# Building kv transposed from split features, and streaming five weight tiles instead of two

## The chip, the cores and the metric

The kernel runs on one core of a Trainium2 chip. The metric is the device time of one execution in microseconds (us). The names of the engines in this document: PE is TensorE (matmuls), PEld its weight loads, DVE is VectorE, ACT is ScalarE, POOL is GpSimd, SP is SyncE, which issues all the DMAs here. SBUF is the on-chip memory of 128 partitions, PSUM the eight banks that PE writes into.

## The reference

It is a linear attention with positive random features, followed by a mixer and an MLP. All is fp32 (U, V and the MLP weights arrive as float64 words).

```python
def phi(x):                                   # q, k: [8, 8, 576, 64], w_phi: [64, 128]
    proj = einsum('bhsd,df->bhsf', x, w_phi)
    proj = proj - max(abs(proj), axis=-1)
    return concatenate([exp(proj), exp(-proj)], axis=-1)     # 256 features
q_p, k_p = phi(q), phi(k)
kv  = einsum('bhsf,bhsd->bhfd', k_p, v)       # [256 features, 64] per head
z   = sum(k_p, axis=2)                        # [256 features] per head
x   = (q_p @ kv) / (q_p @ z + 1e-6)           # then [8, 576, 512]
u   = x + (x^T U V)^T                         # U: [576, 32], V: [32, 576]
out = u + relu(u @ w_ch1) @ w_ch2             # [512, 2048], [2048, 512]
```

The change is about kv and z: for each head, 576 rows of 256 features against 64 columns of v, and the sum of those features.

## The kernel before, in words

**Attention.** Work goes by pairs of heads: eight batches b of four pairs, 32 pairs in all. Of the 576 rows 512 are the main part (NT = 4 tiles of 128) and 64 the tail; the tails of a pair's two heads are done together. Pairs of batches 0 and 1 are unsplit; from batch 2 on (`SPLIT`, L247) a pair is split: q and k are cut into a high part in fp32r, a rounded format, and a low part, the rest in fp32r, and products are made from those parts.

A pair passes through steps (L494 to L519): `s_project_k0` and `s_project_k1` make the k features of the two heads (tiles kp0, kp1: 128 rows x 4 tiles x 256 features, and kpt for the tail); `s_project_q0` and, inside `s_kv0_q1`, `project_q(1)` make the q features, transposed, with a maximum over partitions on POOL (`partition_all_reduce`, L363). kv is built in `kv_tail` (L432) and `kv_main` (L440): v carries a 65th column of ones (`vb`, `vt`, L104 to L115), so that one matmul gives kv and z. In `kv_main` the weights are 128 features (fp32), the moving operand 65 columns of v (fp32): per head 4 tiles x 2 halves of the features = 8 matmuls, all into one PSUM bank, `kv_ps`, held from `kv_tail` to `kv_done` (L447), where DVE copies it out. `s_out0` and `s_out1` (L514, L518) take q's features against kv and divide.

**The mixer and the MLP.** `Tokens` (L527) does U and V for a batch, stores u to DRAM (`u_dram`), and `Mixer.load_blocks` (L600) reads it back in blocks of 32, which `turn_blocks` turns on DVE and splits into `uT_hi` and `uT_lo`. The MLP goes over nine groups g of 512 rows (eight batches and the eight tails), each in sixteen blocks f of 128 hidden units (`Mixer.chunks`, L672): `hidden(f)` is 12 matmuls of 128x512 in fp32r into the bank `ph` (one buffer), which ACT reads as `h_hi` (L624) and then DVE as `h_lo` (L625); `add(f)` is 12 matmuls into four banks `o`. The order is hidden(0), hidden(1), add(0), hidden(2), add(1) and so on.

**The weights.** Each w1 and w2 block is converted once from its float64 words (`convert_block`, L215) while batch 0 and 1 run, split into high and low part and then kept in SBUF, 4 KB a partition for one tile (`home`, a tag per tile). Two blocks, f = 0 and f = 8 (`STREAM`, L188), are also stored to DRAM (`kept`) and later share the home of f = 0: after the last use of the one in a group, `stream` (L198) loads the other from `kept`. Two blocks, f = 8 and f = 15 (`WHOLE`), have homes that other tiles use as well: y of `load_blocks` and the first x.

**The order.** The main loop (L848) runs over pairs: cur is in its output steps, nxt in its feature and kv steps, far has its transfers started, all of them on SP's queue. After each step, `Pace.step` (L719) lets in as many MLP chunks of the batch before as keeps pace: 28 of a group's 32 chunks over 34 steps; the last four (`HELD`) go in while the next group's u is turned. The program is traced in this order. The framework then puts each engine's instructions into a fixed order with a model of their times, and adds the semaphores. Each engine but PE's weight loads runs its own instructions strictly one after another.

PSUM has three banks `at` for attention (projections, kv_ps, xp, transposes), one `ph`, four `o`. Feature tiles have three buffers (`feat`), those of the tail two (`feat_t`), a pair's raw q and k two in all, v's tiles two sets, used by turns.

Of the kernel before, what the change touches and what calls it, by code (L numbers as in the profile page):

```python
# [9 lines left out]
F32 = mybir.dt.float32  # L10
F32R = mybir.dt.float32r
# [10 lines left out]
P = 128  # L22
# [3 lines left out]
def tile_kernel(  # L26
# [46 lines left out]
    def f32(ap):  # L73
        return ap.bitcast(F32)
# [109 lines left out]
    w1_t, w2_t, words, found = {}, {}, {}, {}  # L184
    LAST = NFC - 1

    WHOLE = {LAST: "w_last", 8: "w_late"}
    STREAM = (0, 8)  # L188
    kept = {f: dram.tile([P, 2, 2, C], F32, name=f"kept{f}") for f in STREAM}

    def place(f, dt, shape, name):

        if f in WHOLE:
            both = home.tile([P, 2, *shape], dt, tag=WHOLE[f], name=name)
            return both[:, 0], both[:, 1]
        return [home.tile([P, *shape], dt, tag=f"w{n}_{f}", name=f"{name}_{n}") for n in (1, 2)]

    def stream(n, g, f):  # L198

        to = STREAM[1 - STREAM.index(f)]  # L200
        if g == 0 or g == B and to == 0:
            return
        w = home.tile([P, 2, C], F32R, tag=f"w{n + 1}_0", name=f"w{n + 1}_{to}_{g}")
        nc.sync.dma_start(out=f32(w), in_=kept[to][:, n])
        (w1_t, w2_t)[n][to] = w
# [9 lines left out]
    def convert_block(i):  # L215
        f, n = divmod(i, 2)
        r = convert(words[f][n], f"w{n + 1}_{f}")
        if f not in WHOLE:
            w = home.tile([P, 2, C], F32R, tag=f"w{n + 1}_{f}", name=f"w{n + 1}_{f}")
            split_w((nc.scalar.copy, nc.vector.tensor_copy)[n], r, w)  # L220
        elif n == 0:
            found[f] = r
            return
        else:
            w1_w, w = place(f, F32R, (2, C), f"w_{f}")
            split_w(nc.scalar.copy, found[f], w1_w)
            split_w(nc.vector.tensor_copy, r, w)
            w1_t[f] = w1_w
        (w1_t, w2_t)[n][f] = w
        if f in STREAM:  # L230
            for i in range(2) if f in WHOLE else (n,):
                nc.sync.dma_start(out=kept[f][:, i], in_=f32((w1_t, w2_t)[i][f]))
# [16 lines left out]
    class Pair:  # L249
# [90 lines left out]
        def k_tile(self, n, ng):  # L340
            tag, bufs = ("feat", 3) if ng > 1 else ("feat_t", 2)
            return att.tile([P, ng, 2 * F], F32, tag=tag, bufs=bufs, name=f"kp{self.nm}_{n}")

        def k_features(self, n, k_w, kp):

            ng = kp.shape[1]
# [44 lines left out]
        def project_k_split(self, g):  # L391
# [3 lines left out]
            for s in range(2):  # L395
                pk = self.ps(f"pk{g}{s}_").rearrange("p (t n f) -> p t n f", t=2, n=2)
                for i in range(2):
# [4 lines left out]
                nc.scalar.copy(out=kp[:, ts_, 0:F], in_=pk[:, :, 1, :])  # L402
                nc.vector.tensor_tensor(  # L403
                    out=k_w[:, ts_, :], in0=pk[:, :, 0, :], in1=kp[:, ts_, 0:F], op=ALU.add)
            return self.k_features(g, k_w, kp)

        def project_q_tail(self):
            pq = self.ps("pqt")
# [23 lines left out]
        def kv_tail(self):  # L432
            self.kv_ps = self.ps("kv_ps", True)
            self.kv_v = self.kv_ps[:, 0:4 * (D + 1)].rearrange("p (f h e) -> p f h e", f=2, h=2)
            for f in range(2):
                nc.tensor.matmul(  # L436
                    self.kv_v[:, f, :, :], self.kpt[:, 0, f * F:(f + 1) * F], self.vt,
                    start=(f == 0), stop=False, skip_group_check=True)

        def kv_main(self, g, kp):  # L440
            for t in range(NT):
# [56 lines left out]
        def s_project_k1(self):  # L498
            self.kp1 = self.project_k(1)
            self.project_q_tail()  # L500

        def s_project_q0(self):
            self.qp0 = self.project_q(0)

        def s_kv0_q1(self):
            self.kv_tail()
            self.kv_main(0, self.kp0)
            self.qp1 = self.project_q(1)

        def s_kv1(self):  # L510
            self.kv_main(1, self.kp1)
            self.kv_done()

# [316 lines left out]
    if True:  # L830
# [16 lines left out]
        tk = Tokens(0, x, xt)  # L847
        for n, (b, j) in enumerate(pairs):  # L848

            far = Pair(*pairs[n + 2]) if n + 2 < len(pairs) else None  # L850
            if n < len(LOADS):

# [82 lines left out]
```

## Time and profile before

| what | us |
|---|---|
| median of 3 runs (1226.07 to 1227.72) | 1227.1 |
| the profiled execution | 1233.19 |
| its span, from the first to the last instruction | 1231.4 |
| PE busy in the span | 1204.2 |
| DVE busy | 690.9 |
| ACT busy | 538.2 |
| POOL busy | 203.6 |
| one batch from the third on (382.5 to 516.6) | 134.1 |

Busy time is the union of an engine's instructions. Matmuls are pipelined: their lengths overlap, so what one costs is read from the distance between starts. In rows of the timeline, `x4` means four instructions of one kind merged, and square brackets name the idle time of the engine ahead of the row and what ended it. In rows of groups, the two numbers behind the bar are busy us and the mean ns of one; behind the second bar stands idle time of the engine ahead of them. An unsplit fp32 matmul leaves two records, one for each of its passes.

### The profile page before, as it was taken

How to read it: one execution, taken by the hardware profiler on the slowest of the kernel's cores; microseconds unless marked ns; L12 is line 12 of the kernel's file. 1: busy time of each engine (PE TensorE's matmuls, PEld its weight loads, DVE VectorE, ACT ScalarE, POOL GpSimd, SP SyncE). 2: the span in 40 equal slices, each digit the busy share in tenths (PEclk: the TensorE clock that was granted, in tenths of full speed). 3: DMA queues.
4: the chain of work that ended last, by engine and by line, in shares of the span. 5: the costliest groups of instructions: out<-in, count | busy, mean ns of one | idle time of the engine just before them, and what ended most of it. 6: DMA issues, size and time to landing. Idle time of an engine off the chain costs nothing.

```text
span 1231.4 us, 18285 instructions
## 1 busy us (share of the span) xinstructions
PE 1204.2 (98%) x6667; PEld 1036.6 (84%) x6669; DVE 690.9 (56%) x1517; ACT 538.2 (44%) x1151; POOL 203.6 (17%) x154
## 2 busy tenths in 40 slices
PE   8999998999999999999999999999999999999997
PEld 7887787888888888888888888888888888888886
DVE  5857879775566656665647556655656543312111
ACT  6866678554543444444534444344434431111110
POOL 3533444211110111011111111011201110000000
PEclk9979999999999999999999999999999999999999
DMA  4766221331234213431244123421343015400201
GB/s 133 241 227 208 70 64 30 90 109 25 54 97 116 48 40 91 90 99 30 64 115 111 28 52 86 111 69 26 88 107 98 1 52 150 112 35 1 69 1 35
DMA packets 248345, 100.60 MB, mean 82 GB/s; under 512 B 215360, under 2 KB 227904, under 8 KB 248256
## 3 DMA queue, kind: packets, MB, share of 16 engines
q1 hardware_dynamic: 248256, 99.44, 31.2%
q8 instruction: 53, 0.87, 0.3%
q14 instruction: 36, 0.29, 0.1%
HBM read 78.41 MB, written 20.97 MB: 81 GB/s over the span
## 4 chain that ended last, share of the span: by engine, by line
PE 78%; DVE 8%; SPq 4%; ACT 4%; DMA 4%; issue 1%; POOL 0%; DVEq 0%; ACTq 0%; POOLq 0%
PE ph L619 27%; PE o L640 27%; PE kv_ps L443 7%; PE xp L482 7%; SPq L605 2%; SPq L265 2%; PE pk L399 2%; DVE w L236 1%; PE pp L561 1%; PE kv_ps L436 1%; PE pq L422 1%; DMA raw<-in_q_dram 1%; PE pq L423 1%; PE xpt L469 1%; DMA y<-u_dram 1%
## 5 line engine op out<-in xcount | busy, mean ns | idle before, releaser
L619 PE MATMUL ph<-uT_hi,w 128*128 128x512 f32 x1152 | 389.0, 395 | 4.7 <-DVE h_lo L625 3.3
L640 PE MATMUL o<-w,h_hi 128*128 128x512 f32 x1152 | 327.1, 395 | 3.2 <-ACT h_hi L624 3.2
L619 PEld LDWEIGHTS ph<-uT_hi,w 128*128 128x128 f32 x1152 | 216.2, 188 | 51.2 <-DVE h_lo L625 5.6
L640 PEld LDWEIGHTS o<-w,h_hi 128*128 128x128 f32 x1152 | 211.1, 188 | 45.3 <-ACT h_hi L624 4.9
L619 PE MATMUL ph<-uT_lo,w 128*128 128x512 f32 x576 | 225.1, 391 | 0.0
L624 ACT ACTIVATE h_hi<-ph 128x512 fp32r<-128x512 f32 x144 | 85.9, 596 | 272.0 <-PE ph L619 261.0
L625 DVE SCALAR_TENSOR_TENSOR h_lo<-ph,h_hi 128x512 fp32r<-128x512 f32 x144 | 98.6, 685 | 176.6 <-ACT h_hi L624 175.4
L640 PE MATMUL o<-w,h_lo 128*128 128x512 f32 x576 | 191.9, 395 | 0.6 <-DVE h_lo L625 0.6
L363 POOL PARTITION_ALL_REDUCE qp<-qp x64 | 126.7, 1980 | 286.6 <-ACT qp L362 268.1
L443 PEld LDWEIGHTS kv_ps<-vb,kp 128*128 128x128 f32 x1024 | 126.6, 195 | 2.8
L482 PEld LDWEIGHTS xp<-kv,qp 128*128 128x128 f32 x1024 | 124.1, 194 | 4.8 <-DVE kp L403 0.9
L619 PEld LDWEIGHTS ph<-uT_lo,w 128*128 128x128 f32 x576 | 108.3, 188 | 21.3 <-DVE uT_lo L244 0.6
L443 PE MATMUL kv_ps<-vb,kp 128*128 128x65 f32 x1024 | 126.0, 274 | 0.1
L482 PE MATMUL xp<-kv,qp 128*128 128x65 f32 x1024 | 124.0, 274 | 0.6 <-DVE kp L403 0.6
L640 PEld LDWEIGHTS o<-w,h_lo 128*128 128x128 f32 x576 | 105.4, 188 | 21.6 <-DVE h_lo L625 1.3
L353 ACT ACTIVATE kp<-kp 128x512 f32<-128x512 f32 x64 | 40.4, 632 | 132.9 <-DVE kp L350 83.4
L363 POOL PARTITION_ALL_REDUCE qp_t<-qp_t x32 | 27.2, 851 | 403.2 <-ACT qp_t L362 401.0
L319 DVE TENSOR_TENSOR T<-raw,T 64x512 fp32r<-64x512 f32 x96 | 68.5, 714 | 33.6 <-ACT T L318 31.1
L315 DVE STREAM_TRANSPOSE raw<-raw 128x512 f32<-128x512 f32 x48 | 34.1, 711 | 80.3 <-DMA raw<-in_q_dram 36.8
L318 ACT CAST T<-raw 64x512 fp32r<-64x512 f32 x96 | 59.3, 618 | 33.9 <-PE pq L423 23.4
L365 ACT ACTIVATE qp<-qp 128x512 f32<-128x512 f32 x64 | 40.4, 631 | 59.8 <-DVE qp L364 59.5
L146 POOL INT64_ADD w_ab<-w_ab x32 | 44.1, 1377 | 76.0 <-DVE w_ab L142 40.4
(128 smaller groups left out, 1357.1 us busy)
## 6 DMA issues: line engine op xcount, KB each, us to landing
words<-in_moe_w_ch_dram SPq DMA_DIRECT2D x32, 512.0 KB, 8.0
w<-kept SPq DMA_DIRECT2D x30, 512.0 KB, 4.1
vb<-in_v_dram SPq DMA_DIRECT2D x64, 128.0 KB, 2.5
u_dram<-x SPq DMA_DIRECT2D x32, 256.0 KB, 2.2
st<-u_dram SPq DMA_DIRECT2D x16, 512.0 KB, 4.0
out_dram<-st SPq DMA_DIRECT2D x32, 256.0 KB, 2.3
y<-u_dram SPq DMA_DIRECT2D x112, 64.0 KB, 2.4
raw<-in_k_dram SPq DMA_DIRECT2D x192, 32.0 KB, 2.0
```

Of the source, the lines that this page charges most:

```text
L146: nc.gpsimd.int64_add(a64, a64, b64)
L318: nc.scalar.copy(out=m[here, s, :], in_=x_[here])
L319: nc.vector.tensor_sub(m[there, s, :], x_[here], f32(m[here, s, :]))
L353: nc.scalar.activation(out=kp[:, :, 0:F], in_=kp[:, :, F:2 * F], func=AF.Exp)
L363: nc.gpsimd.partition_all_reduce(qp[:, 0, :], qp[:, 1, :], P, ReduceOp.absmax)
L365: nc.scalar.activation(out=qp[:, 0, :], in_=qp[:, 1, :], func=AF.Exp)
L443: nc.tensor.matmul(self.kv_v[:, f, g, :], kp[:, t, f * F:(f + 1) * F], self.vb[:, g, t, :], start=False, stop=(t == NT - 1), skip_group_ch ...
L482: nc.tensor.matmul(xv[:, c, :], qp[:, f, c * P:(c + 1) * P], self.kv[:, f, c // 2 if self.split else s, :], start=(f == 0), stop=(f == 1))
L619: nc.tensor.matmul(ph, w1_part(f, l, c), r[:, c, :], start=(n == 0), stop=(n == 3 * NCC - 1))
L624: on_act = nc.scalar.activation(out=h_hi, in_=ph, func=AF.Relu)
L625: on_dve = nc.vector.scalar_tensor_tensor(out=h_lo, in0=ph, scalar=0.0, in1=f32(h_hi), op0=ALU.max, op1=ALU.subtract)
L640: nc.tensor.matmul(self.o[t], l[:, cs], w2_t[f][:, r, :], start=(f == 0 and n == 0), stop=(f == NFC - 1 and n == 2))
```

## The change

For split pairs, kv is built the other way round, as 64 rows of v against 256 moving features, and in fp32r parts:

- v is split into high and low part, side by side as 128 weight columns (`v_parts`); the features into `khi` (ACT) and `klo` (DVE) (`k_parts`).
- `kv_turned` streams the features' two parts past v's two parts: per head 4 tiles x 2 parts = 8 matmuls of 128x256 into one bank `kt`. Its upper and lower 64 rows, from v's high and low part, are added into `kvT`.
- `kv_end`, at the head of the next pass of the main loop, turns `kvT` back with two transposes on PE, does the tail (`kv_tail`, which stood in `s_kv0_q1`), copies `kv_ps` out and adds the turned kv and the sums.
- The sums z of the main rows, which the ones column gave, come from `k_sums`: two adds on DVE, a sum over partitions on POOL, and a trip through DRAM (`zd`) that turns a row of 256 sums per head into columns (`k_sums_turned`).

Room for these tiles comes from the weights: five blocks (0, 3, 6, 9, 12) instead of two now share the home of f = 0 and are streamed one after another; the homes that blocks 3, 6 and 9 have during batch 0's group (`late0` to `late5`) then serve the tiles above. `w_late` holds block 12 instead of 8. Unsplit pairs run as before.

```diff
-    WHOLE = {LAST: "w_last", 8: "w_late"}
-    STREAM = (0, 8)
+    WHOLE = {LAST: "w_last", 12: "w_late"}
+    STREAM = (0, 3, 6, 9, 12)
...
+    def place_of(n, f):
+        if f in STREAM[1:]:
+            return f"late{2 * STREAM.index(f) - 2 + n}"
+        return f"w{n + 1}_{f}"
...
     def stream(n, g, f):
-        to = STREAM[1 - STREAM.index(f)]
+        to = STREAM[(STREAM.index(f) + 1) % len(STREAM)]
...
+        def k_sums(self, g, kp):
+            if g == 0:
+                self.zs = home.tile([P, 2, 2, 2 * F], F32, tag="late2", name=f"zs{self.nm}")
+                self.zd = dram.tile([2, 2 * F], F32, tag="zd", bufs=2, name=f"zd{self.nm}")
+            zs = self.zs[:, g]
+            nc.vector.tensor_add(zs, kp[:, 0:2, :], kp[:, 2:4, :])
+            nc.vector.tensor_add(zs[:, 0, :], zs[:, 0, :], zs[:, 1, :])
+            nc.gpsimd.partition_all_reduce(zs[:, 1, :], zs[:, 0, :], P, ReduceOp.add)
+            nc.sync.dma_start(out=self.zd[g:g + 1, :], in_=zs[0:1, 1, :])
+
+        def k_sums_turned(self):
+            self.zc = small.tile([P, 2, 2], F32, tag="zc", bufs=2, name=f"zc{self.nm}")
+            nc.sync.dma_start(
+                out=self.zc.rearrange("p g n -> p (g n)"),
+                in_=self.zd.rearrange("g (n f) -> f (g n)", f=F))
+
+        def k_parts(self, g, kp):
+            hi = home.tile([P, NT, 2 * F], F32R, tag=f"late{5 * g}", name=f"khi{self.nm}_{g}")
+            lo = home.tile([P, NT, 2 * F], F32R, tag="late1", name=f"klo{self.nm}_{g}")
+            nc.scalar.copy(out=hi, in_=kp)
+            nc.vector.tensor_sub(lo, kp, f32(hi))
+            return hi, lo
+
+        def v_parts(self):
+            self.v_hl = home.tile([P, 2, NT, 2 * D], F32R, tag="late3", name=f"v_hl{self.nm}")
+            src = self.vb[:, :, :, 0:D]
+            nc.scalar.copy(out=self.v_hl[:, :, :, 0:D], in_=src)
+            nc.vector.tensor_sub(
+                self.v_hl[:, :, :, D:2 * D], src, f32(self.v_hl[:, :, :, 0:D]))
+
+        def kv_turned(self, g, parts):
+            kt = self.kt = self.ps(f"kt{g}_")
+            for t in range(NT):
+                for n in range(2):
+                    nc.tensor.matmul(
+                        kt[:, 0:2 * F], self.v_hl[:, g, t, :], parts[n][:, t, :],
+                        start=(t == 0 and n == 0), stop=(t == NT - 1 and n == 1))
+            if g == 0:
+                self.kvT = home.tile([P, 2, 2 * F], F32, tag="late4", name=f"kvT{self.nm}")
+            r_ = slice(g * D, (g + 1) * D)
+            nc.scalar.copy(out=self.kvT[r_, 1, :], in_=kt[D:2 * D, 0:2 * F])
+            nc.vector.tensor_add(self.kvT[r_, 0, :], kt[0:D, 0:2 * F], self.kvT[r_, 1, :])
+
+        def kv_end(self):
+            if not self.split:
+                return
+            kb = self.kt[:, 2 * F:4 * F]
+            for f in range(2):
+                nc.tensor.transpose(
+                    out=kb[:, f * P:(f + 1) * P], in_=self.kvT[:, 0, f * F:(f + 1) * F],
+                    identity=ident)
+            self.kv_tail()
+            self.kv = small.tile([P, 2, 2, D + 1], F32, tag="kv", bufs=1, name=f"kv{self.nm}")
+            nc.vector.tensor_copy(out=self.kv, in_=self.kv_v)
+            nc.vector.tensor_add(
+                self.kv[:, :, :, 0:D], self.kv[:, :, :, 0:D],
+                kb.rearrange("p (f h d) -> p f h d", f=2, h=2))
+            nc.vector.tensor_add(
+                self.kv[:, :, :, D:D + 1], self.kv[:, :, :, D:D + 1],
+                self.zc.rearrange("p g n -> p n g").unsqueeze(3))
...
                 nc.vector.tensor_tensor(
                     out=k_w[:, ts_, :], in0=pk[:, :, 0, :], in1=kp[:, ts_, 0:F], op=ALU.add)
-            return self.k_features(g, k_w, kp)
+            self.k_features(g, k_w, kp)
+            self.k_sums(g, kp)
+            return kp
...
         def s_project_k1(self):
             self.kp1 = self.project_k(1)
             self.project_q_tail()
+            if self.split:
+                self.v_parts()
 
         def s_project_q0(self):
             self.qp0 = self.project_q(0)
+            if self.split:
+                self.parts0 = self.k_parts(0, self.kp0)
 
         def s_kv0_q1(self):
+            if self.split:
+                self.k_sums_turned()
+                self.kv_turned(0, self.parts0)
+                self.qp1 = self.project_q(1)
+                self.parts1 = self.k_parts(1, self.kp1)
+                return
             self.kv_tail()
             self.kv_main(0, self.kp0)
             self.qp1 = self.project_q(1)
 
         def s_kv1(self):
+            if self.split:
+                self.kv_turned(1, self.parts1)
+                return
             self.kv_main(1, self.kp1)
             self.kv_done()
...
         for n, (b, j) in enumerate(pairs):
 
+            cur.kv_end()
             far = Pair(*pairs[n + 2]) if n + 2 < len(pairs) else None
```

More of the change, by code (lines that the diff above doesn't have):

```diff
@@ L195, in place @@
             return both[:, 0], both[:, 1]
-        return [home.tile([P, *shape], dt, tag=f"w{n}_{f}", name=f"{name}_{n}") for n in (1, 2)]
+        return [home.tile([P, *shape], dt, tag=place_of(n, f), name=f"{name}_{n}") for n in (0, 1)]
     def stream(n, g, f):
-        to = STREAM[1 - STREAM.index(f)]
+        to = STREAM[(STREAM.index(f) + 1) % len(STREAM)]
         if g == 0 or g == B and to == 0:
@@ L218, in convert_block @@
         if f not in WHOLE:
-            w = home.tile([P, 2, C], F32R, tag=f"w{n + 1}_{f}", name=f"w{n + 1}_{f}")
+            w = home.tile([P, 2, C], F32R, tag=place_of(n, f), name=f"w{n + 1}_{f}")
             split_w((nc.scalar.copy, nc.vector.tensor_copy)[n], r, w)
@@ L437, in kv_tail @@
                     self.kv_v[:, f, :, :], self.kpt[:, 0, f * F:(f + 1) * F], self.vt,
-                    start=(f == 0), stop=False, skip_group_check=True)
+                    start=(f == 0), stop=self.split and f == 1, skip_group_check=True)
         def kv_main(self, g, kp):
```

## The prediction

> **What bounds the kernel now.** I read the page's busy times first, then busy time by windows, then the timeline of TensorE, then the waits.
>
> ```profile
> span 1231.4 us, 18285 instructions
> PE 1204.2 (98%) x6667; PEld 1036.6 (84%) x6669; DVE 690.9 (56%) x1517; ACT 538.2 (44%) x1151; POOL 203.6 (17%) x154
> ```
>
> The profiled execution took 1233.2 us, 1.8 us more than its span and 6.1 us more than the median of the runs (1227.1); I sum against 1233.2 and take 6.1 off at the end. A busy PE need not be a full one, so I ask stage by stage (columns: window, length, then busy PE, PEld, DVE, ACT, POOL).
>
> ```profile
> 80.00:248.00 168.00, 157.57 (x885) 133.18 (x886) 135.43 (x263) 118.62 (x234) 63.95 (x44) 0.99 0.33 97
> 382.50:516.60 134.10, 133.75 (x768) 116.74 (x767) 81.48 (x185) 59.89 (x133) 18.94 (x12) 1.00 0.33 76
> 650.70:784.80 134.10, 133.44 (x766) 116.24 (x766) 80.54 (x183) 59.51 (x132) 18.95 (x12) 1.00 0.32 75
> ```
>
> From about 248 us on a batch (four pairs of heads, sixteen MLP blocks) takes 134.1 us, and PE is idle in 0.35 to 0.66 us of it. DVE is busy 60%, ACT 45%. So in that stage PE time removed is time removed, until another engine takes PE's place. The timeline shows what a pair's kv costs there (start, length, instruction; starts follow each other without gaps, lengths overlap).
>
> ```profile
> 594.15 0.61 PE L436 MATMUL kv_ps<-vt,kp_t 128*128 128x130 f32 x4
> 594.60 1.90 PE L443 MATMUL kv_ps<-vb,kp 128*128 128x65 f32 x16
> 596.30 0.48 PE L422 MATMUL pq<-T,w_hl 128*128 128x512 f32 x1
> 596.62 0.40 PE L423 MATMUL pq<-T,w_hl 128*128 128x512 f32 x1
> 596.85 1.89 PE L443 MATMUL kv_ps<-vb,kp 128*128 128x65 f32 x16
> 598.55 0.48 PE L619 MATMUL ph<-uT_hi,w 128*128 128x512 f32 x1
> 598.87 0.40 PE L619 MATMUL ph<-uT_lo,w 128*128 128x512 f32 x1
> ```
>
> Eight program matmuls of one head are sixteen records: plain fp32 runs each in two passes. One head takes 596.30 - 594.60 = 1.70 us, the tail 0.45. The first 128x512 after such a stretch takes 0.32 us to the next start where the usual step is 0.23 (596.62 to 596.85): 0.09 us per stretch. A pair's kv: 0.45 + 2 x 1.70 + 2 x 0.09 = 4.03 us.
>
> **The change, PE part.** kv_turned takes 8 matmuls of 128x256 in fp32r per head; kv_end adds two 128x128 transposes; the two tail matmuls move there unchanged. The same shapes run already:
>
> ```profile
> 603.41 0.64 PE L399 MATMUL pk<-w_hl,T 128*128 128x256 f32 x4
> 603.89 0.40 PE L640 MATMUL o<-w,h_lo 128*128 128x512 f32 x1
> 244.17 0.60 PE L593 MATMUL pt<-ident,x 128*128 128x128 f32 x4
> 244.52 0.48 PE L577 MATMUL vp<-pst,v_all 128*128 128x512 f32 x1
> ```
>
> (603.89 - 603.41) / 4 = 0.12 us a matmul, single records, so 16 are 1.92 us. A transpose is (244.52 - 244.17) / 4 = 0.09 us; I take 0.10. One fp32 stretch is left: 0.09. Together 1.92 + 0.20 + 0.45 + 0.09 = 2.66 us, saved 1.37 us a pair. Batches 2 to 7 are split, 24 pairs: **32.9 us off PE**. A batch becomes 134.1 - 5.5 = 128.6 us if nothing else takes over.
>
> [...]
>
> ```profile
> L399 PEld LDWEIGHTS pk<-w_hl,T 128*128 128x128 f32 x192 | 31.2, 189 | 4.2
> ```
>
> **DVE, ACT, POOL.** Prices of the added work (count | busy us, mean ns):
>
> ```profile
> L350 DVE TENSOR_TENSOR kp<-kp,mk 128x512 f32<-128x512 f32 x48 | 33.1, 690 | 1.2
> L548 DVE TENSOR_TENSOR xs<-x,xs 128x256 fp32r<-128x256 f32 x64 | 27.2, 470 | 7.7 <-ACT xs L547 7.5
> L403 DVE TENSOR_TENSOR kp<-pk,kp 128x256 f32<-128x256 f32 x96 | 37.4, 409 | 2.0 <-ACT kp L402 2.0
> L456 DVE TENSOR_SCALAR den<-xp 128x4 f32<-128x4 f32 x64 | 10.2, 160 | 27.9 <-PE xp L482 27.2
> L353 ACT ACTIVATE kp<-kp 128x512 f32<-128x512 f32 x64 | 40.4, 632 | 132.9 <-DVE kp L350 83.4
> L402 ACT COPY kp<-pk 128x256 f32<-128x256 f32 x96 | 33.3, 371 | 35.0 <-PE pk L399 34.8
> L363 POOL PARTITION_ALL_REDUCE qp<-qp x64 | 126.7, 1980 | 286.6 <-ACT qp L362 268.1
> L363 POOL PARTITION_ALL_REDUCE qp_t<-qp_t x32 | 27.2, 851 | 403.2 <-ACT qp_t L362 401.0
> ```
>
> From 256 to 512 columns DVE adds about 0.27 us and ACT 0.26, so 128x1024 is near 1.23 and 1.15 us. DVE per pair: sums 2 x (0.69 + 0.47), lo parts 2 x 1.23, v's lo 0.69, kvT adds 2 x 0.41, the two last adds 0.41 + 0.16 (the copy out of kv_ps was there before): 6.9 us, 27 a batch. ACT: hi parts 2 x 1.15, v's hi 0.63, kt copies 2 x 0.37: 3.7 us, 15 a batch. POOL: two reductions of 256 columns, between 0.85 and 1.98, by the slope 1.23 us each: 10 a batch. New shares of 128.6 us: DVE (80.5 + 27) / 128.6 = 84%, ACT 58%, POOL 22%. No engine passes PE, but DVE takes its instructions in order and comes near.
>
> What PE loses by that is the one large unknown, and it sits at the single ph bank: hidden(f+1) may not start before h_hi (ACT) and h_lo (DVE) of f have read ph. The pure MLP at the end shows the cover that add(f-1) gives alone:
>
> ```profile
> 1121.13 0.39 PE L619 MATMUL ph<-uT_hi,w 128*128 128x512 f32 x1
> 1122.18 0.69 DVE L625 SCALAR_TENSOR_TENSOR h_lo<-ph,h_hi 128x512 fp32r<-128x512 f32 x1 [5.88 <-ACT h_hi L624]
> 1124.07 0.62 PE L619 MATMUL ph<-uT_hi,w 128*128 128x512 f32 x2
> ```
>
> h_lo ends at 1122.87, the next hidden starts at 1124.07: 1.2 us spare, more wherever a pair's matmuls lie between. One queued lo part (1.23 us) uses that up. The bounds: a batch now, at 60% DVE, idles 0.35 us of PE, so nothing; the stretch from 80 to 248 us, at 81% DVE, idles 168.0 - 157.6 = 10.4 us, 6.2%, and over 6 x 128.6 us that would be 48 us. Part of those 10.4 us stands on this very mechanism:
>
> ```profile
> 152.25 2.12 PE L640 MATMUL o<-w,h_hi 128*128 128x512 f32 x8 [1.48 <-ACT h_hi L624]
> 192.26 0.50 PE L619 MATMUL ph<-uT_hi,w 128*128 128x512 f32 x1 [1.12 <-DVE h_lo L625]
> 203.91 0.50 PE L619 MATMUL ph<-uT_hi,w 128*128 128x512 f32 x1 [1.62 <-DVE h_lo L625]
> ```
>
> These make 4.2 us, 2.5%, or 19 us over the six batches; there weight conversions also fill ACT and POOL (71% and 38%), which they do not later. I take half, **10 us**, and keep 0 and 48 for the range. Behind each lo part on DVE wait h_lo, the k features and the q subtraction; behind that, PE.
>
> [...]
>
> ```profile
> 620.26 1.94 POOL L363 PARTITION_ALL_REDUCE qp<-qp  x1 [3.70 <-PE ph L619]
> 621.54 0.72 DVE L548 TENSOR_TENSOR xs<-x,xs 128x256 fp32r<-128x256 f32 x2
> 685.08 0.76 DVE L548 TENSOR_TENSOR xs<-x,xs 128x256 fp32r<-128x256 f32 x2 [0.47 <-ACT xs L547]
> ```
>
> Beside the reduction two such adds take 0.72 us, without one 0.76. I add nothing.
>
> **DMA and SP.** Per batch six more 512 KB loads of streamed weights, per pair two 1 KB writes of the sums and one read of 512 single elements; before the split, six more stores to kept.
>
> ```profile
> w<-kept SPq DMA_DIRECT2D x30, 512.0 KB, 4.1
> SPq L265 <- DVE T L319: 302.6, 41, 18.4
> SPq L291 <- PE kv_ps L436: 5.6, 7, 1.1
> 642.20 8.29 SPq L605 DMA_DIRECT2D y<-u_dram  x16
> ```
>
> A streamed tile has three blocks of 134.1 / 16 = 8.4 us to arrive: 25 us, less the 2.7 us of a hidden. SP's longest stall, 18.4 us, and the landing, 4.1, just fit. The element read has as many pieces as one y transfer (512), which costs 8.29 / 16 = 0.52 us of SP; it is needed two steps later. kv_tail moves behind kv_turned to the head of the loop, ahead of far's transfers; it issues none itself, but far's load of vt, into the same buffer, now waits for it, and behind that on SP stand vb and the next raws. Today that wait is 1.1 us at most; those loads are needed a pair later. kpt, too, keeps one of its two feat_t buffers until then, and the next pair's k tail, which follows at once, takes it over: DVE can wait there for the tail's 0.45 us of PE. Nothing for all this, 0 to 5 us; for the stores and the changed order of conversion before 248 us, where PE does wait, **2 us** (0 to 6).
>
> kv's way to s_out0 gets longer by the transposes, two PSUM adds and the tail, about 1.3 us after the last kt, covered by one MLP block and the next pair's k projection; at the last pair that cover is thin, so 0 to 2 us once, taken at 0.
>
> **Sum.** 1233.2 - 32.9 + 10 + 2 = 1212 us for a profiled execution, less 6.1: **1206 us**. I call 0.2% (2.5 us) what a measurement of this kernel can tell from no change.
>
> **The rivals.** (1) Slower: DVE in front of ph. Six batches have 96 hidden blocks; above 32.9 / 96 = 0.34 us of extra PE idle at each, the gain is gone. At the full 6.2% of the early stretch it is 1227.1 - 32.9 + 48 + 2 = 1244 us. For it: 84% against 81%, and a spare of 1.2 us against a lo part of 1.23. Against it: only 4.2 of the 10.4 us belong to this wait, and the timeline changes between pair and block every few microseconds (L399 to L640 above), so other PE work often stands ready. Chance 0.17, of which 0.06 lies within 0.2% of today. (2) Weights late: two of SP's longest stalls on top of each other make 2 x 18.4 + 4.1 - 22.4 = 18.5 us once per batch, 111 us in six: about 1317. The queue's order would have to put the load behind two blocked raws; chance 0.03. (3) The weight loads of kv_turned are not hidden: 16 x 0.19 = 3.0 us more per pair, so 1.7 slower than now instead of 1.4 faster, 24 x 3.0 = 73 us above the forecast: 1279. The L399 rows speak against it; chance 0.02. (4) Nothing is given back: 1227.1 - 32.9 = 1194, part of the forecast's own range.
>
> **How the numbers follow.** The forecast, 1194 to 1224, has 0.78. Slower is 0.11 + 0.03 + 0.02 = 0.16, within 0.2% 0.06. The range goes from 1193 (all of the gain, rounding aside) to 1229, where 0.16 is left out above and a little below.
>
> **What would show it.** Right: L443 keeps only the unsplit pairs, 256 records; kt runs as 384 single records at 0.12 us; a batch lasts 128.6 to 132 us; DVE is busy over 80% of it. PE's idle time should have h_lo (L625) or h_hi as releaser and grow to 1 to 3 us a batch. Wrong: kt spaced at 0.2 us or more; PE idle above 5.5 us a batch; PE waiting for w or for kvT, khi or klo instead of h_lo.

## The result, and the profile after

The change makes the kernel slower. Before: 1226.6 us (median of 4 runs, 1225.9 to 1227.7). After: 1265.4 us (median of 4, 1263.6 to 1269.1). The ratio is 1.030, 95% interval 1.0274 to 1.0326. The forecast of 1206 us missed by 59 us, and its range ended at 1229.

The profiled execution took 1269.1 us, with a span of 1267.3 us, 35.9 longer than before. The page of after, the span, the busy times and the row of granted clock, and below it that row of before:

```profile
span 1267.3 us, 18400 instructions
PE 1216.5 (96%) x6331; PEld 1032.7 (81%) x6333; DVE 865.7 (68%) x1781; ACT 622.1 (49%) x1271; POOL 315.5 (25%) x202
PEclk9979998989996999989998999889998999999999
```

```profile
PEclk9979999999999999999999999999999999999999
```

PE is busy longer than before, although it has fewer matmuls. The rows of clock say why: in many more slices than before the clock is not full. Busy time by windows, the same stretches of time as in the prediction, shows it too (behind the engines' columns stands the granted clock):

```profile
80.00:248.00 168.00, 157.78 (x847) 132.25 (x848) 137.10 (x265) 120.07 (x234) 67.66 (x46) 0.96 0.37 111
382.50:516.60 134.10, 126.55 (x648) 106.91 (x648) 104.93 (x222) 71.67 (x149) 35.80 (x19) 0.91 0.38 93
650.70:784.80 134.10, 131.23 (x696) 112.03 (x696) 106.38 (x216) 69.69 (x143) 34.16 (x18) 0.97 0.39 97
```

In the second row PE is idle for 7.5 us where it was idle 0.35, and runs 648 records where it ran 768, at a clock of 0.91. DVE has gone from 81 to 105 us of 134. The added operations themselves cost what was forecast. Groups by line:

```profile
L387 PE MATMUL kt<-khi,v_hl 128*128 128x256 f32 x192 | 49.2, 283 | 1.2 <-DVE tail_T L303 1.1
L516 PE MATMUL kv_ps<-vb,kp 128*128 128x65 f32 x256 | 33.4, 283 | 0.1
L372 DVE TENSOR_TENSOR klo<-kp,khi 128x1024 fp32r<-128x1024 f32 x48 | 60.9, 1268 | 2.5 <-PE kt L387 2.2
L356 DVE TENSOR_TENSOR zs<-kp 128x512 f32<-128x512 f32 x48 | 33.1, 689 | 16.8 <-ACT kp L425 16.5
L358 POOL PARTITION_ALL_REDUCE zs<-zs x48 | 106.6, 2221 | 414.0 <-DVE zs L357 373.6 <-DVE den L530 38.6 <-PE pp L647 1.7
```

Only POOL's reduction was mis-sized, 2.22 us against 1.23. The matmuls of `kv_turned` follow each other at 0.12 us, from PE's timeline:

```profile
531.26 0.28 PE L387 MATMUL kt<-khi,v_hl 128*128 128x256 f32 x1
531.37 0.28 PE L387 MATMUL kt<-klo,v_hl 128*128 128x256 f32 x1
...
531.97 0.28 PE L387 MATMUL kt<-khi,v_hl 128*128 128x256 f32 x1
532.09 0.28 PE L387 MATMUL kt<-klo,v_hl 128*128 128x256 f32 x1
```

So PE's work fell, and time came in elsewhere. Where is seen at the boundary between two groups of the MLP. First the kernel before, PE's timeline around the first hidden of group 4, at 657.38:

```profile
654.53 2.11 PE L640 MATMUL o<-w,h_hi 128*128 128x512 f32 x8 [0.66 <-ACT h_hi L624]
656.48 1.07 PE L640 MATMUL o<-w,h_lo 128*128 128x512 f32 x4
657.38 0.39 PE L619 MATMUL ph<-uT_hi,w 128*128 128x512 f32 x1
```

The last `o` of the old group runs straight into the first `ph` of the new one: while u makes its trip through DRAM (the y transfers begin at 642.20, a row of the prediction) old blocks keep PE busy. Such a boundary in after, into group 3, on PE and then on SP:

```profile
534.87 1.15 PE L726 MATMUL o<-w,h_lo 128*128 128x512 f32 x4
...
536.20 0.48 PE L470 MATMUL pk<-w_hl,T 128*128 128x256 f32 x2
539.91 0.80 PE L470 MATMUL pk<-w_hl,T 128*128 128x256 f32 x2 [3.23 <-DVE kv L408]
541.37 3.52 PE L555 MATMUL xp<-kv,qp 128*128 128x65 f32 x16
544.64 0.77 PE L705 MATMUL ph<-uT_hi,w 128*128 128x512 f32 x1
```

```profile
533.75 0.49 SPq L665 DMA_DIRECT2D u_dram<-xt  x1
534.51 8.37 SPq L691 DMA_DIRECT2D y<-u_dram  x16
```

The old group ends at 536.0, when the y transfers have just begun. PE is left with pieces of pairs, waits 3.23 us for kv_end's add, and then runs at half clock (0.50 from 539.91 to 544.64): the 16 `xp` records (128x65) take 3.52 us, where 16 `kv_ps` records of that size took 1.90 in the kernel before, a row of the prediction. The first `ph` comes 8.6 us after the last `o`.

To add this up, I give each matmul its usual distance to the next start (0.227 us for 128x512, 0.118 for 128x256, and so on) and call that work. What a distance has above it by more than 0.12 us is a pause, and in stretches at half clock the longer distance (0.427 us for 128x512) is a term of its own. The window goes from group 1's first hidden to group 7's; 23 of the 24 split pairs build their kv in it. The last column counts, from the same timeline, the old group's blocks (hidden or add) still to come at the batch's last mixer matmul (`vp`), at the boundaries into groups 2 to 6. Before was run again beside each set of experiments (medians 1226.6 to 1232.6 us), and each ratio is against those runs.

| kernel | ratio to before (95%) | window | work | pauses | half clock | blocks left |
|---|---|---|---|---|---|---|
| before | 1 | 793.3 | 772.2 | 3.4 | 0 | 5.2 |
| after | 1.030 (1.027 to 1.033) | 821.7 | 743.4 | 32.3 | 32.9 | 0 to 1.1 |
| e1_stream_only | 1.012 (1.009 to 1.014) | 800.3 | 770.3 | 12.3 | 0 | 5.2 |
| e2_kb_on_act | 1.074 (1.071 to 1.078) | 878.3 | 746.6 | 67.1 | 54.8 | 0 |
| e3_no_sums | 1.028 (1.025 to 1.030) | 819.3 | 746.1 | 35.4 | 23.7 | 0 to 1.2 |
| e4_end_in_kv1 | 1.024 (1.022 to 1.027) | 811.7 | 743.2 | 30.4 | 24.8 | 0 to 1.0 |
| e5_held8 | 1.022 (1.018 to 1.027) | 820.8 | 743.4 | 39.9 | 22.4 | 0 to 3.1 |
| e6_held12 | 1.022 (1.018 to 1.026) | 817.5 | 743.4 | 31.2 | 29.4 | 0 to 3.1 |
| e7_before_held8 | 1.008 (1.005 to 1.011) | 794.9 | 772.9 | 3.4 | 1.8 | 7.7 to 12.3 |
| e8_before_held0 | 1.037 (1.033 to 1.042) | 846.0 | 775.6 | 29.2 | 24.5 | 0 |
| f1_j23 | 1.022 (1.017 to 1.027) | 822.6 | 757.4 | 29.2 | 21.6 | 1.8 to 3.7 |
| f2_j123 | 1.029 (1.025 to 1.032) | 818.7 | 749.6 | 40.4 | 15.4 | 1.8 |
| f3_j01 | 1.026 (1.022 to 1.029) | 823.2 | 759.0 | 31.2 | 14.6 | 3.4 to 4.3 |
| f4_warm | 1.040 (1.037 to 1.043) | 840.8 | 773.2 | 45.8 | 9.3 | 2.0 to 4.3 |
| g1_hold4 | 1.033 (1.028 to 1.038) | 827.0 | 745.2 | 49.6 | 17.2 | 4.0 |
| g2_hold8 | 1.041 (1.038 to 1.045) | 842.2 | 743.4 | 53.4 | 30.0 | 8.0 |
| g3_hold8_kv1 | 1.032 (1.029 to 1.036) | 828.2 | 743.2 | 47.9 | 19.4 | 8.0 |
| h1_light | 1.013 (1.008 to 1.017) | 807.8 | 746.1 | 28.1 | 20.1 | 0 to 3.4 |
| h2_short | 1.037 (1.033 to 1.040) | 836.8 | 738.4 | 49.0 | 36.3 | 0 to 3.1 |
| h3_both | 1.002 (0.999 to 1.004) | 795.2 | 738.0 | 29.5 | 10.5 | 1.6 to 4.3 |

The first two rows are the balance: 28.8 us of PE work gone, 28.9 us of pauses and 32.9 us of half clock come in. What stands in no column, steps a little above their usual distance, among them those at switches between fp32 and fp32r, falls from 17.7 to 13.1 us, so the window grows by 28.4 us; the rest of the 35.9 us between the two profiled executions lies ahead of it (5.9) and behind it (1.6). Of after's pauses DVE ends 28.0 us and ACT 2.3, of before's 1.6 and 1.8. All but 0.5 us of after's pauses in this window, and all of its half clock, lie within 25 us of a group's first hidden.

### The profile page after: what moved, and what is told of

It reads as the page before. It is cut to its first block, busy times and chain, and to the rows that moved or that the text cites. A ratio compares the mean times of both kernels' runs of the same rounds, so it can differ in the third digit from the quotient of the medians.

```text
span 1267.3 us, 18400 instructions
## 1 busy us (share of the span) xinstructions
PE 1216.5 (96%) x6331; PEld 1032.7 (81%) x6333; DVE 865.7 (68%) x1781; ACT 622.1 (49%) x1271; POOL 315.5 (25%) x202
## 4 chain that ended last, share of the span: by engine, by line
PE 69%; DVE 14%; SPq 5%; ACT 5%; DMA 4%; issue 3%; POOL 1%; DVEq 0%; ACTq 0%; POOLq 0%
PE ph L705 25%; PE o L726 25%; PE xp L555 7%; PE kt L387 3%; SPq L271 2%; SPq L691 2%; DVE T L325 2%; PE pk L470 2%; DVE w L242 2%; DMA y<-u_dram 1%; PE pp L647 1%; PE xpt L542 1%; DMA u_dram<-x 1%; ACT w_ab L138 1%; PE kv_ps L516 1%
## 5 line engine op out<-in xcount | busy, mean ns | idle before, releaser
L705 PE MATMUL ph<-uT_hi,w 128*128 128x512 f32 x1152 | 392.2, 401 | 1.9 <-DVE h_lo L711 1.2
L726 PE MATMUL o<-w,h_hi 128*128 128x512 f32 x1152 | 315.4, 398 | 3.8 <-ACT h_hi L710 3.6
L705 PE MATMUL ph<-uT_lo,w 128*128 128x512 f32 x576 | 230.3, 400 | 4.4 <-DVE uT_lo L250 4.3
L358 POOL PARTITION_ALL_REDUCE zs<-zs x48 | 106.6, 2221 | 414.0 <-DVE zs L357 373.6
L726 PE MATMUL o<-w,h_lo 128*128 128x512 f32 x576 | 183.6, 394 | 0.0
L434 POOL PARTITION_ALL_REDUCE qp<-qp x64 | 132.6, 2073 | 152.6 <-ACT qp L433 152.4
L555 PEld LDWEIGHTS xp<-kv,qp 128*128 128x128 f32 x1024 | 135.8, 210 | 4.8 <-ACT qp L436 0.7
L555 PE MATMUL xp<-kv,qp 128*128 128x65 f32 x1024 | 137.3, 292 | 0.5 <-DVE kp_t L421 0.3
L325 DVE TENSOR_TENSOR T<-raw,T 64x512 fp32r<-64x512 f32 x96 | 77.0, 802 | 13.8 <-ACT T L324 11.0
L372 DVE TENSOR_TENSOR klo<-kp,khi 128x1024 fp32r<-128x1024 f32 x48 | 60.9, 1268 | 2.5 <-PE kt L387 2.2
L473 ACT COPY kp<-pk 128x256 f32<-128x256 f32 x96 | 34.3, 371 | 52.4 <-PE pk L470 52.0
```

Source lines behind the costliest of these rows:

```text
L325: nc.vector.tensor_sub(m[there, s, :], x_[here], f32(m[here, s, :]))
L358: nc.gpsimd.partition_all_reduce(zs[:, 1, :], zs[:, 0, :], P, ReduceOp.add)
L372: nc.vector.tensor_sub(lo, kp, f32(hi))
L434: nc.gpsimd.partition_all_reduce(qp[:, 0, :], qp[:, 1, :], P, ReduceOp.absmax)
L555: nc.tensor.matmul(xv[:, c, :], qp[:, f, c * P:(c + 1) * P], self.kv[:, f, c // 2 if self.split else s, :], start=(f == 0), stop=(f == 1))
L705: nc.tensor.matmul(ph, w1_part(f, l, c), r[:, c, :], start=(n == 0), stop=(n == 3 * NCC - 1))
```

## The experiments

The theories, in the order in which they came up. A, **the bank**: kv_end's adds come late on DVE and hold the bank kt, for which pk waits. B, **the amount** of new work on DVE. C, **the stream** of weights. D, **POOL**: its reduction slows DVE's instructions. E, **the cover**: the old group's blocks run out before u is back. F, **the place**: only pairs beside the boundary hurt. G, **the chain**: the pairs' steps as a chain last longer than PE's work, wherever the blocks stand.

### One part of the change alone, or one part undone

**e1_stream_only.** The five streamed blocks, with kv built as before.

```diff
-            if self.split:
-                self.kv_turned(1, self.parts1)
-                return
...
-            cur.kv_end()
```

> Only the weights change: five blocks share one home and are streamed, kv is built as before. Theory A (place: at the batch boundary an overfull DVE frees the banks of attention late, PE pauses, and the pause halves its granted clock): this kernel has none of the new DVE work, so about the time of before, 1225 to 1231 us, with a granted clock of 0.99. Theory B (amount: all of the 27 us of DVE work per batch counts, wherever it stands): the same. Theory C (the streamed weights or SP's fuller queue are late): at least a third of the 39 us lost, 1240 us or more, and PE waits for w.

1242.5 us against 1228.5, ratio 1.0116. Theory C is right in part: the stream, with its stores and the changed order of conversion, costs 14 us. Only 7.0 us of that show in the window (800.3 against 793.3). There is no gap at the boundary and no half clock in the window. The pauses are of the kind that the prediction looked for, at h_hi and h_lo. Waits of PE, then of SP, in e1:

```profile
PE o L712 <- ACT h_hi L696: 5.6, 7, 1.1
PE ph L691 <- DVE h_lo L697: 4.2, 5, 2.4
```

```profile
SPq L271 <- DVE T L325: 144.5, 37, 18.4
SPq L210 <- PE pk L470: 112.7, 16, 11.2
SPq L210 <- PE o L712: 82.1, 21, 9.4
```

L210 is the load of a streamed weight. It waits on SP, in these rows up to 11.2 us, until PE has let go of the old block, and what stands behind it waits too, for SP issues nothing in that time; in before the largest of such waits stood at L265, a row of the prediction. PE never waits long for a weight, so where these 14 us arise in the chain is argued, not shown.

**e2_kb_on_act.** ACT copies the turned kv out of the bank kt, DVE adds from the copy.

```diff
+            nc.scalar.copy(out=self.kvT[:, 1, :], in_=kb)
             self.kv_tail()
...
-                kb.rearrange("p (f h d) -> p f h d", f=2, h=2))
+                self.kvT[:, 1, :].rearrange("p (f h d) -> p f h d", f=2, h=2))
```

> The changed kernel, but ACT copies the turned kv out of its bank right after the transposes, so the bank no longer waits for the last adds on DVE (L408 of the changed kernel). DVE keeps its work. Theory A: the pauses of 3.2, 1.95, 1.1 and 1.1 us ahead of the k projection go, with two to four of the half-clock stretches behind them: 1240 to 1256 us. Theory B: within 4 us of the changed kernel's 1265. Theory C: no change.

1319.6 us, ratio 1.074: 54 us slower than after, where theory A expected a gain. The wait of pk for kv's add, 7.4 us in after, is gone, and the time rose all the same: the bank is not what PE lacks. One more step in the way of kv, through a second queue, doubled the pauses; this speaks for a chain (G), which came later. But the copy also holds `kvT` until DVE's add has read it, so the run does not show a chain by itself.

**e3_no_sums.** The sums z of the main rows are left out: `k_sums`, `k_sums_turned` and the add of zc.

```diff
-            self.k_sums(g, kp)
             return kp
```

> Leaves out the sums z of the main rows of split pairs (two DVE adds and one POOL reduction per head, the trip through DRAM, the last small add): 2.3 us less DVE and 4 us less POOL work per pair, a third of what was added to DVE. Theory B: a third to a half of the 39 us lost and of the 33 us given back, 1235 to 1245 us. Theory A: less, since the bank still waits behind the group's last adds, 1245 to 1262 us. A rival D (POOL's reduction slows the DVE instructions beside it, 28 us in all of stretched instructions): as low as 1235 us, and DVE's stretched instructions fall back from 57 us to about 30.

1263.5 us, ratio 1.028: no different from after. A third of DVE's new work and all of POOL's new work is gone, 9 us of DVE a batch, and nothing came of it. D falls as the main cause. B in its simple form, time in proportion to DVE's work, falls as well.

**e4_end_in_kv1.** kv_end right behind kv_turned(1), so that kt isn't held across the boundary.

```diff
+                self.kv_end()
                 return
...
-            cur.kv_end()
```

> The changed kernel, but the turning back, the tail and the last adds stand right behind kv_turned of the second head instead of at the head of the next loop pass. The work is the same, only its place in the order differs: at the batch boundary it now stands ahead of the last chunks of the group and of the turning of the next blocks. Theory A: the pauses ahead of the k projection go, 1235 to 1255 us. Theory B: 1260 us or more, with new waits of PE for kvT.

1259.3 us, ratio 1.024, some 7 us better than after, with intervals that almost meet. What A names is there, but small.

### The cover at the boundary

Theory E rests on the number of blocks kept back (`HELD`), so it can be tried on both kernels with one number.

```diff
-    HELD = 4
+    HELD = 8
```

> The changed kernel with eight instead of four MLP chunks held back for the batch boundary. Theory E (cover: in the changed kernel the last matmul of a group's MLP ends 7 to 17 us before the next group's first hidden, where before it ended at the very moment; nothing but the thin attention work is left for PE there, so it pauses and its granted clock halves): the gap falls under 3 us at most boundaries, the half-clock stretches from 248 to 1000 us fall from 74 us to under 25, and the time to 1205 to 1235 us. Theory A/B (banks freed late by a DVE at 84%, amount): gap or no gap, DVE's work is the same: 1255 us or more.

> The same with twelve chunks held. Theory E: no gaps at all, 1200 to 1230 us, unless the many chunks at one place starve the steps between; a theory of amount: 1255 us or more.

> The kernel before with eight chunks held: the control for the two runs above. There is no gap to fill in the kernel before, so by theory E 1224 to 1234 us. If it becomes faster by more than 5 us, holding more chunks helps for a reason of its own.

> The kernel before with no chunk held: takes the cover away without any of the change. Theory E: gaps of 8 to 15 us between the groups, half-clock stretches at each boundary, 1245 to 1290 us, the same picture as in the changed kernel. If cover is not the cause: within 8 us of 1228.

In after, 8 and 12 give 1257.3 and 1257.4 us (ratio 1.022 both), a gain of 9 us. In before, 8 costs 0.8%, though its window grows by only 1.6 us. And with 0, before takes 1276.1 us, ratio 1.037: without any part of the change it has 29 us of pauses, 24.5 of half clock and gaps of 10 to 12 us from the last `o` to the first `ph`. Taking the cover away is thus enough to make the same picture. Its row of granted clock and its largest wait of PE:

```profile
PEclk9999999999998999999998999889999999999999
```

```profile
PE pk L399 <- DVE x L578: 4.9, 5, 1.3
```

But that E is sufficient doesn't make it the cause in after. With 8 or 12 kept back there, only 0 to 3.1 blocks were left at the last `vp`: the framework's order still lets the MLP run ahead of the pairs' steps. At two of the five boundaries the gap did close, and the pauses of the whole window stayed at 39.9 and 31.2 us.

**f1_j23, f2_j123, f3_j01.** Only some of a batch's pairs turned, the others as before, with the stream in all of them.

```diff
+            self.turned = self.split and j in (2, 3)
...
-            if not self.split:
+            if not self.turned:
                 return
             kb = self.kt[:, 2 * F:4 * F]
```

> The changed kernel, but only the third and fourth pair of each split batch build kv the new way; the first two, whose features are made while the next group's blocks are turned on DVE, build it as before. Twelve pairs save 1.37 us of PE each, 16 us. Theory F (place: what costs is the new DVE work among the turning and splitting of the blocks at the batch boundary, where DVE is full, PE runs out of other work and its clock halves): the boundaries look like those of the kernel with the streamed weights alone (1242 us), so 1222 to 1232 us. Theory B (amount, wherever it stands): half way between 1242 and 1265, 1248 to 1258 us, the same as the mirror run on the first two pairs.

> The same with the second to fourth pair (18 pairs, 25 us saved). The second pair's sums and parts fall into the turning too, the first pair's last adds do not. Theory F: between, 1228 to 1250 us. Theory B: 1255 to 1262 us.

> The mirror: only the first and second pair of each split batch build kv the new way. The same amount of new work as with the third and fourth, the same 16 us of PE saved. Theory F: the boundaries stay as bad as in the changed kernel, 1250 to 1270 us, at least 20 us above the run with the third and fourth. Theory B: equal to that run within 4 us.

1261.3, 1268.0 and 1263.9 us, ratios 1.022, 1.029 and 1.026. Half of the turned pairs cost as much as all, and those beside the boundary no more than the others: F falls. In f3 the old group's last `o` again meets the first `ph`, and the pauses stay at 31 us. So they don't come from the gap alone.

**f4_warm.** Six small matmuls on constant data behind each of the four `turn_blocks`, to keep the clock up.

```diff
                 mix(c % 2)
+                keep_busy(6)
```

> The changed kernel with 24 dummy matmuls (bf16, 128x512) at each batch boundary from batch 2 on, six behind each turned block: work for PE that waits for nothing but its bank. It tells the halved clock apart from the pauses themselves. If the halved clock is most of the loss (88 us at half speed cost 44 us): the half-clock stretches from 248 us on shrink by half or more and the time falls to 1235 to 1255 us in spite of 5 us of dummy work per boundary. If the pauses themselves are the loss: 1265 to 1290 us.

1281.5 us, ratio 1.040. Half clock falls from 32.9 to 9.3 us, pauses rise from 32.3 to 45.8, and the fillers take 6 x 24 x 0.216 = 31 us themselves. The time lies where it was expected if the pauses themselves are the loss. Less the fillers the window would be some 12 us shorter than after's (840.8 - 31 = 810). So part of the half clock stood where PE would have waited anyway; the 32.9 us are not all to be had.

### Cover or chain

**g1_hold4, g2_hold8, g3_hold8_kv1.** The last four or eight blocks of a group may go only behind the batch's last `vp` on PE. g3 holds eight back and has the edit of e4 as well.

```diff
-            tk.up(NT)
+            last = tk.up(NT)
             mix(len(todo) - HELD)
+            hold[:] = [todo[0][0].__self__, last]
...
+                if hold and fn.__self__ is hold[0]:
+                    with tc.issue_after(hold[1]):
+                        fn(f)
```

> The kernel after, but the last four blocks of each group may be issued on PE only behind the next batch's last mixer matmul (vp of the tail). Cover theory (the MLP ran ahead by the issue order alone): four blocks, 10.7 us, are there to cover u's trip, the gap from the last o to the first hidden falls from 7 to 17 us to under 4 us, pauses and half clock fall by half or more, time 1215 to 1240. Chain theory (the pairs' steps on DVE and at the banks last longer than PE's work): PE pauses earlier in the batch instead, pauses more than 25 us from a boundary appear where there are none now, time 1255 to 1275.

> The same with eight blocks held behind the last vp (21 us of cover). Cover theory: no gap, no half clock, time 1205 to 1230, better than with four. Chain theory: 1255 to 1285, as more of the MLP is withheld from the pairs' steps, PE pauses of 10 us or more a batch away from the boundary.

> Eight blocks held, and kv_end right behind kv_turned(1) (as in e4). Cover theory: as with eight held, 0 to 6 us better, 1200 to 1228. Chain theory: 1250 to 1280.

1273.4, 1281.8 and 1273.1 us, ratios 1.033, 1.041 and 1.032. All three times lie where G expected them, and none near E's. In g2 all eight blocks stand behind the last `vp`, u is turned 1.7 us or more before the first hidden (0.5 us or more in before), and the pauses near the boundary fall to 1.3 to 3.5 us a group (2.5 to 8.2 in after). In exchange PE pauses 6.7 to 9.1 us in each of groups 1 to 5 farther away, where after has 0.5 at most. Blocks kept back are not harmful by themselves: in e7, with 7.7 to 12.3 left, before has no more pauses than without. So a lack of cover alone (E) is not the cause. For G the evidence is g2; in g1 and g3 only 10 and 16 us of some 49 stand farther than 25 us from a boundary. The longest pauses of g2 in group 3, on PE and then on DVE:

```profile
659.53 0.39 PE L647 MATMUL pp<-xs,u_all 128*128 128x256 f32 x1 [0.73 <-DVE xs L634]
664.79 2.37 PE L663 MATMUL vp<-pst,v_all 128*128 128x512 f32 x4 [4.87 <-DVE pst L651]
```

```profile
657.83 0.42 DVE L634 TENSOR_TENSOR xs<-x,xs 128x256 fp32r<-128x256 f32 x1
658.16 1.32 DVE L634 TENSOR_TENSOR xs<-xt,xs 128x256 fp32r<-128x256 f32 x1
659.40 0.70 DVE L321 STREAM_TRANSPOSE raw<-raw 128x512 f32<-128x512 f32 x1
660.03 0.65 DVE L435 TENSOR_TENSOR qp<-qp 128x512 f32<-128x512 f32 x1
660.60 1.21 DVE L372 TENSOR_TENSOR klo<-kp,khi 128x1024 fp32r<-128x1024 f32 x1
661.84 0.69 DVE L712 SCALAR_TENSOR_TENSOR h_lo<-ph,h_hi 128x512 fp32r<-128x512 f32 x1
662.45 0.41 DVE L394 TENSOR_TENSOR kvT<-kt,kvT 64x256 f32<-64x256 f32 x1
662.88 1.40 DVE L325 TENSOR_TENSOR T<-raw,T 64x512 fp32r<-64x512 f32 x2
664.32 0.42 DVE L651 TENSOR_TENSOR pst<-pp,pst 32x256 fp32r<-32x256 f32 x1
```

The last `pp` ends at 659.9. `pst`, 0.42 us long, is the next link of u's chain, and it comes 4.4 us later, at the end of a queue on DVE without a hole above 0.04 us: in it stand klo and kvT, 1.6 us that the change put there, and others that an earlier backlog pushed along. In the kernel before, the same instruction came with DVE idle ahead of it:

```profile
624.16 0.69 DVE L364 TENSOR_TENSOR qp<-qp 128x512 f32<-128x512 f32 x1
625.12 0.42 DVE L565 TENSOR_TENSOR pst<-pp,pst 32x256 fp32r<-32x256 f32 x1 [0.27 <-ACT pst L564]
```

### What makes the chain long

**h1_light, h2_short, h3_both.** h1 takes most of DVE's new work away, e3's sums among it, and keeps the matmuls. h2 cuts the way of kv behind kvT. h3 is both.

```diff
-            nc.vector.tensor_sub(lo, kp, f32(hi))
-            return hi, lo
+            return hi, hi
...
-            nc.vector.tensor_sub(
-                self.v_hl[:, :, :, D:2 * D], src, f32(self.v_hl[:, :, :, 0:D]))
+            nc.scalar.copy(out=self.v_hl[:, :, :, D:2 * D], in_=src)
```

```diff
-                nc.tensor.transpose(
-                    out=kb[:, f * P:(f + 1) * P], in_=self.kvT[:, 0, f * F:(f + 1) * F],
-                    identity=ident)
...
-                self.kv[:, :, :, 0:D], self.kv[:, :, :, 0:D],
-                kb.rearrange("p (f h d) -> p f h d", f=2, h=2))
```

> The kernel after with most of VectorE's added work left out: the low parts of the features and of v are not computed (the high part is streamed twice, so PE's matmuls stay as they are; v's second half is a copy on ACT), and the sums z of the main rows are left out with their reduction and their DMAs. VectorE loses 2 x 1.27 + 0.69 + 2 x 1.16 + 0.16 = 5.7 of 6.9 us a pair. Theory of the amount (VectorE's queue is the chain): pauses and half clock go, PE's saving and the streaming's cost remain, 1195 to 1220. Theory of the way (kt, kvT, transposes, bank held): pauses stay above 25 us, time 1245 to 1265.

> The kernel after with the way of kv cut: the two transposes and the add from the bank kt are left out, so that kvT goes nowhere, kt is free right after its last read and kv holds only the tail's part and the sums. VectorE loses 0.41 of 6.9 us a pair, PE 0.2. Theory of the way: pauses and half clock fall to a third, 1205 to 1230. Theory of the amount: 1245 to 1262.

> Both left out. If one of the two is the cause alone, this is within 8 us of the one that took the cause away; if they add up, it is lower than each, 1190 to 1210. If it still stays above 1235, neither is the cause, and what is left is the streaming and the order of issue.

h1: 1246.0 us against 1231.1, ratio 1.0125. h2: 1275.5, ratio 1.0365. h3: 1233.1, ratio 1.0018 (0.9994 to 1.0041). None of the three came out as one theory alone had it. By its time and its 28 us of pauses h1 stands at the lower edge of what the theory of the way expected; but from after to h1 the ratio falls by 0.0175, 21 us, more than by any other single edit, and what this edit takes away is five sixths of DVE's new work. In the window it is mainly the half clock that fell, by 12.8 us; the pauses fell by 4.2. h2 is above both expectations, and h3 a little below the 1235 us from which neither would be the cause. DVE's busy time is back near before's 80 of 134 us, and pauses are left all the same. The windows of h1 and of h3:

```profile
517.00:651.00 134.00, 129.52 (x694) 110.65 (x693) 84.07 (x189) 74.53 (x154) 19.95 (x12) 0.97 0.39 96
```

```profile
517.00:651.00 134.00, 130.16 (x703) 109.50 (x702) 85.25 (x194) 74.59 (x157) 19.46 (x12) 1.00 0.41 100
```

The way of kv behind kvT costs nothing while DVE's queue is long: cutting it alone (h2) made it no faster, 1.037 against 1.030. With DVE's queue short it costs 13 us more (h1 to h3); some 5 us of them are PE's own transposes, by the prediction's 0.10 us each. With both gone the kernel is as fast as before, not faster, although PE has 34 us less to do: 26 us of added pauses and 10.5 of half clock take that. e1 found 9 us of added pauses with the stream alone; the other 27 us are not explained by any run here. The trace of h3 shows a rival that no run tests. Its largest waits of PE are for ACT:

```profile
PE o L710 <- ACT h_hi L694: 7.0, 10, 1.2
PE vp L647 <- ACT qp L419: 3.1, 4, 0.8
```

Of the pauses in h3's window ACT ends 13.6 us and DVE 13.3. ACT is busy 427 us there, against 341 in before: its new work is left in h3, and no edit takes it away.

## Why the prediction was wrong

**PE's saving** was right, and for the reason given: 28.8 us of matmuls and some 2 us at switches, at the prediction's 0.09 us for each of 23 pairs (163 between fp32 and fp32r in the window, 248 in before), where the window's 23 pairs at 1.37 make 31.5, at 0.12 us a matmul and with 256 records left at the old line. The rival that the weight loads stand outside their matmuls (1279) is out: in after each of the 384 matmuls of `kt` has a load of its own, 0.19 us long (L387), and the matmuls follow each other at 0.12 us, as those of pk did.

**The prices on DVE and ACT** were right to 0.1 us an instruction (klo 1.27 against 1.23). POOL's reduction was taken at 1.23 us and took 2.22. To add nothing to DVE beside POOL was too quick: summed over all instructions that lasted more than 0.15 us above the median of their kind, DVE lost 29.5 us in before and 57.1 in after, 45.5 of these beside a reduction. One such instruction is the 1.32 us in the rows of g2 above, beside a reduction from 658.00 to 659.90, against 0.42 of the row before it. In e3, without the new reductions, the sum falls to 39.9 us and the time stays, so it isn't what made the kernel slower.

**The step that failed is what PE loses by DVE**, "it sits at the single ph bank", taken at 10 us. It failed in three ways.

- The place. I looked for the wait at h_lo and h_hi in every block. In after those waits take 1.2 and 3.6 us in all, in before 3.3 and 3.2; the large ones hang on kv_end's add, on uT_lo and on xt. Waits of PE in after:

```profile
PE pk L470 <- DVE kv L408: 7.4, 4, 3.2
PE ph L705 <- DVE uT_lo L250: 4.3, 5, 1.4
PE pkt L444 <- DVE xt L664: 3.8, 2, 2.0
PE o L726 <- ACT h_hi L710: 3.6, 5, 1.5
...
PE ph L705 <- DVE h_lo L711: 1.2, 1, 1.2
```

  A block of the MLP has other matmuls beside it, as I argued. A batch's u has only a handful of old blocks: mixer, DRAM, turn, split are a chain of short instructions, and those on DVE queue there anew. I read shares of batches and never asked what runs while this chain runs. The cover was in the trace of before: 5.2 blocks, 14 us, for the 17 to 19 us from the last `vp` to the last `uT_lo`. In after that stretch takes 16 to 20 us, no longer than before, but 0 to 1.1 blocks are left for it; what was lost lies ahead of it, in the order of the old blocks and in the pairs' steps and the mixer, as `pst` in g2.
- The size. Pauses grew by 28.9 us, not 10 + 2.
- The clock. A pause was priced at its own length. After such pauses the clock was halved (0.50) for 6.8 to 23.9 us at a time: 32.9 us in the window, a term that the sum did not have at all. f4 shows that not all of it would have been won back.

**Rival 1** (DVE in front of PE) had the right engine and the sign, with a chance of 0.17 and a top of 1244. Its test, 0.34 us at each hidden, was the wrong one. **The signs** I named told it: the 0.12 us of kt and the 256 records came; a batch, from first hidden to first hidden in groups 1 to 5, took 134 to 143 us and not 128.6 to 132; DVE ended at 78 and 79% in the windows shown, not above 80; and of the signs of being wrong, PE's idle time above 5.5 us came in one of the two windows (7.5, and 2.9 in the other), with releasers other than h_lo and h_hi in front.

**DMA and SP** were taken at nothing, 0 to 5, and the stores and the order of conversion at 2; e1 measured 14 us for the two together. I had asked only whether a weight lands in time. The load also waits for its place at the head of SP's one queue, up to 15.0 us in e1, and holds up what is behind it. **kv_end's longer way**, taken at 0 to 2 us once, is some 8 us beside its transposes where DVE's queue is short (h1 to h3), and not seen beside a long one (h2).

To explain are 39 us of loss and 31 of saving that did not come, 70 in all. Runs of their own show 14 for the stream, 21 for five sixths of DVE's work, and 8 for the way, without its transposes, once that work is gone. These are not independent, and some 27 us are left. What keeps 27 us of pauses and half clock in h3 (ACT's new work is the untested rival), and why half of the pairs turned cost as much as all (f1, f3), stays open.

## What to carry to other kernels

Before work moves from the busiest engine to a second one, look not only at the second one's share but at the longest serial chain that passes through its queue, and count what else the busy engine has to do while that chain runs: here 14 us of old blocks in before, of which after had almost none left when the chain needed them. A pause of TensorE should be priced with the half clock behind it, here 32.9 us beside 32.3 of pauses. And where the second queue is busy some 80% of the time, as DVE here, taking a third of the new work away may show nothing (e3) and five sixths may show 21 us (h1), so a single small undoing is weak evidence against an amount.

## What the runs showed of the hardware

In after, half clock also followed pauses of 2.0 us and less. Its windows just ahead of and in two such stretches:

```profile
672.00:675.50 3.50, 1.35 (x9) 1.13 (x9) 3.05 (x9) 1.22 (x3) 0.00 (x0) 1.00 0.80 125
675.50:682.30 6.80, 6.80 (x26) 5.92 (x25) 6.22 (x16) 4.01 (x10) 0.00 (x0) 0.50 0.69 149
805.00:808.60 3.60, 1.65 (x14) 1.41 (x13) 3.54 (x7) 2.25 (x4) 0.00 (x0) 1.00 0.77 228
808.60:818.80 10.20, 9.07 (x35) 8.15 (x36) 8.02 (x19) 3.63 (x9) 0.00 (x0) 0.50 0.69 110
```

Ahead of the first PE was idle 2.15 of 3.5 us, of the second 1.95 of 3.6, with no single pause above 2.0 us, and the half clock lasted 6.8 and 10.2 us. At 194.2 us one pause of 1.5 us was followed by 3.4 us of half clock, at 392.2 a row of pauses of 0.3 to 1.3 us by 23.9. They were not always followed by it: in before, pauses of 1.48 and 1.62 us (at 152.25 and 203.91, rows of the prediction) were followed by none, the clock from 152 to 156 and from 203 to 208 us being 1.00. What decides between the two is not shown here.
